# A state-space layer with a GeGLU branch on one core: last token tile projected in 384 and 128 columns, tile 0 normalised and transposed in halves, first w_gate chunk from the ScalarE queue

## Chip, cores, metric

One core of a Trainium2 chip. The metric is device time in microseconds (us) of one execution, the median of several. The profile is taken of one execution; its span runs from the first to the last instruction of the core and is about 1.8 us shorter than the device time of the same execution.

## The reference

```python
x = A_x                                   # [1, 2048, 512] bf16
xn = layernorm(x)                         # no weights, eps 1e-5
# A: diagonal complex state space, 512 states, over 2048 tokens
h_t = Lam_bar * h_{t-1} + B_bar @ xn_t ;  yA = 2 * Re(C @ h) + xn * Dskip
# B: GeGLU, hidden width 1376
yB = (gelu(xn @ w_gate) * (xn @ w_up)) @ w_down
out = x + yA + yB                         # bf16
```

## The kernel before

Tokens are handled in 4 blocks of 512 (`NB`), each of 4 tiles of 128. The kernel writes down operations with the buffers that they read and write; a list scheduler in the same file orders VectorE (DVE), ScalarE (ACT) and GpSimd (POOL) by modelled times, while TensorE (PE) and the sync queue (SP) keep the order of the program. Only the start (block 0) and the end (the last tile of block 3) matter for this change. "First projections" below means the products of block 0 with the first five chunks of 128 hidden columns of w_gate and w_up (`GU_first`). Its "second half" is the part for tiles 2 and 3. The cut below is abridged: most buffers, durations and dependencies are left out.

```python
for j in range(4):
    ld_x0(j)                                   # 128 KB each, sync queue
ld_w(WG, WGc, ins["B_w_gate"], 0)              # first chunk, 384 columns, 384 KB
ld_w(WU, WUc, ins["B_w_up"], 0)
ld_w(WG, WGc, ins["B_w_gate"], 1); ld_w(WU, WUc, ins["B_w_up"], 1)
...                                            # cut: three 1 KB parameter loads on the ScalarE queue
def LN(b, js=range(4), on_act=False, after=()):
    for j in js:
        V(bn_stats(ST[tt], X[tt]), after); V(bn_aggr(MVt[b][j], ST[tt]))
    ACT(sbq = var + eps); ACT(qb = Sqrt(sbq)); V(rq = 1 / qb)
    for j in js: V(XN[tt] = (X[tt] - mn) * rq)            # 512 columns at a time
def TR0(j, eng):                               # 4 PE transposes of tile j into one bank, one copy of 512 columns
    ...
def GU_first(fts, early, single):              # fts 0..4, early 0..2; u = 0 is w_gate, u = 1 is w_up
    for u in range(2):
        for ft in early:
            mm(ft, u, 0, 1)                    # tile 0: four matmuls of 128 columns
            if single and u == 0 and ft == 1:
                TR0(1, "A")                    # transposes of tile 1, copied by ScalarE
    for ft in early:
        for u in range(2):
            mm(ft, u, 1, 2)                    # tile 1
        evac(ft, 0)                            # Gelu on ACT, copy on ACT, product on DVE
    mm(late[0], 0, 0, 2)
    TR0(2, "V"); TR0(3, "A")
    ...                                        # cut: the other late chunks
    for ft in fts:
        for u in range(2): mm(ft, u, 2, 4)     # second half: tiles 2 and 3, 256 columns
        evac(ft, 1)
def DN(b, split=False):                        # 128 tokens x 512 columns per tile j
    ...
    for j in range(4):
        seed(j)                                # ACT puts x into the bank
        hidden(j); states(j)                   # 11 + 8 matmuls of 512 columns
        store(j)                               # DVE: bank + XD -> OUTB, then one store of 128 KB
...
nwarm = 11
PE(fwarm)                                      # nwarm matmuls of 512 columns on zeros, ahead of the first transposes
LN(0, [0], True); TR0(0, "V"); fill(4); params()     # params: one small PE transpose, then tiny operations
LN(0, [1], True, [GATE["bnag"]]); LN(0, [2, 3], True, [GATE["evT"]])
load_B(); GU_first(range(5), range(3), True)
...                                            # cut: blocks 0 to 3
GU(3, ...); DN(2); DN(3)
```

Of the kernel before, what the change touches and what calls it, by code (L numbers as in the profile page):

```python
# [61 lines left out]
class Op:  # L62
    __slots__ = ("id", "eng", "fn", "dur", "deps", "kind", "reads", "writes", "start", "finish",
                 "sem", "val", "users", "tag", "issue")

    def __init__(self, id_, eng, fn, dur, kind, reads, writes, tag):
        self.id, self.eng, self.fn, self.dur, self.kind = id_, eng, fn, float(dur), kind
        self.reads, self.writes, self.tag = reads, writes, tag
        self.deps, self.users = [], []
        self.start = self.finish = None  # L70
        self.sem = None
        self.val = None
        self.issue = DMA_ISSUE


class Sched:
# [134 lines left out]
    def _forward(self, prio):  # L211
# [13 lines left out]
        def rdy_time(op):  # L225
            return max([d.finish + LAT(d, op) for d in op.deps], default=0.0)

# [136 lines left out]
def build(nc, ins, out):  # L364
    with ExitStack() as es:
# [48 lines left out]
        XTk = [[Buf("XT%d_%d" % (b, i), "xt", 4 * b + i, 4 * b + i + 1) for i in range(4)] for b in range(NB)]  # L414
        XT0 = XTk[0]
        XTr = lambda b: XTk[b]
        WRM = A.alloc("WRM", [128], BF16)
# [52 lines left out]
        for j in range(4):  # L470
            ld_x0(j)
        ld_w(WG, WGc, ins["B_w_gate"], 0)
        ld_w(WU, WUc, ins["B_w_up"], 0)
# [43 lines left out]
        SCR = A.alloc("SCR", [1], F32)  # L517
        ACT(lambda e: e.activation(SCR.ap, HALF.ap[:, 0:1], ACTF.Sqrt), 200, [HALF, IOTJ], [SCR], "sqrt0")
        POOL(lambda e: e.memset(HR.ap, 0.0), 300, [], HRp, "hr0")
# [74 lines left out]

        def LN(b, js=range(4), on_act=False, after=()):
            j0, j1 = js[0], js[-1] + 1
            mn, sbq, qb, rq = (cols(t, b, j0, j1) for t in (MN, SBQ, QB, RQ))
            mv = Buf("MV%d_%d" % (b, j0), "sb", MVt[b][j0].lo, MVt[b][j1 - 1].hi, MV[b].ap[:, j0:j1])
            for j in js:
                tt = 4 * b + j  # L600
                V(lambda e, tt=tt: e.bn_stats(ST[tt].ap, X[tt].ap), d_dve_1x(512), [X[tt]], [ST[tt]], "bnst", after)  # L601
                GATE["bnag"] = V(lambda e, tt=tt, j=j: e.bn_aggr(MVt[b][j].ap, ST[tt].ap), D_TINY, [ST[tt]], [MVt[b][j]], "bnag")
            POOL(lambda e: e.tensor_copy(mn.ap, mv.ap[:, :, 0]), 200, [mv], [mn], "mn")
            if on_act:
                ACT(lambda e: e.activation(sbq.ap, mv.ap[:, :, 1], ACTF.Identity, bias=EPS.ap), d_act(4), [mv, EPS, SCR], [sbq], "sbq")  # L605
                ACT(lambda e: e.activation(qb.ap, sbq.ap, ACTF.Sqrt), d_act(4), [sbq], [qb], "sqrt")
            else:
                V(lambda e: e.tensor_scalar(sbq.ap, mv.ap[:, :, 1], EPS_BF16, None, ALU.add), D_TINY, [mv], [sbq], "sbq")
                POOL(lambda e: e.tensor_tensor(qb.ap, sbq.ap, HALF.ap[:, 0:j1 - j0], ALU.pow), 1100, [sbq, HALF], [qb], "pow")
            V(lambda e: e.reciprocal(rq.ap, qb.ap), 150, [qb], [rq], "rq")  # L610
            for j in js:
                tt = 4 * b + j
                xs = XN[tt % 8]
                V(lambda e, tt=tt, j=j, xs=xs: e.tensor_scalar(  # L614
                    xs.ap, X[tt].ap, mn.ap[:, j - j0:j - j0 + 1], rq.ap[:, j - j0:j - j0 + 1], ALU.subtract, ALU.mult),
                  d_dve_ts4x(512), [X[tt], mn, rq], [xs], "ln_n")

# [7 lines left out]

        def TR0(j, eng):
            if not TBANK:
                TBANK.extend([next_bank(), next_bank()])
            bank = TBANK[j % 2]
            pt = PS[bank].bitcast(BF16)  # L630

            def f(e):
                ins_ = None
                for q in range(KD):
                    ins_ = e.transpose(pt[:, 128 * q:128 * (q + 1)], XN[j].ap[:, 128 * q:128 * (q + 1)], IDN.ap)  # L635
                return ins_
            PE(f, 75.0 * KD, [XN[j], IDN], [BANK[bank]], "T0")
            dst = XNT[0].ap[:, :, 128 * j:128 * (j + 1)]
            src = pt[:, 0:512].rearrange("p (q t) -> p q t", q=KD)
            if eng == "A":  # L640
                ACT(lambda e: e.activation(dst, src, ACTF.Copy), d_act(512), [BANK[bank]], [XT0[j]], "evT")
            else:
                GATE["evT"] = V(lambda e: e.tensor_copy(dst, src), 420, [BANK[bank]], [XT0[j]], "evT")  # L643

# [67 lines left out]
        def GU_first(fts, early, single):  # L712
# [14 lines left out]

            def evac(ft, h):
                bank, c0 = banks[h][ft], 256 * h
                GATE["nh"] = kk = (GATE["nh"] + 1) % 3  # L730
                GATE["last_gelu"] = ACT(lambda e: e.activation(GG[kk].ap[:, 0:256], PS[bank][:, 0:256], ACTF.Gelu_apprx_tanh),  # L731
                                        d_act(256), [BANK[bank]], [GG[kk]], "gelu")
                ACT(lambda e: e.activation(UPB[kk].ap[:, 0:256], PS[bank][:, 256:512], ACTF.Copy),
                    d_act(256), [BANK[bank]], [UPB[kk]], "evU")
                V(lambda e: e.tensor_tensor(HTt[0][ft].ap[:, c0:c0 + 256], GG[kk].ap[:, 0:256], UPB[kk].ap[:, 0:256], ALU.mult),  # L735
                  d_dve_tt2x(256), [GG[kk], UPB[kk]], [HTt[0][ft]], "hmul")

            for u in range(2):
                for ft in early:
                    mm(ft, u, 0, 1)  # L740
                    if single and u == 0 and ft == 1:
                        TR0(1, "A")
            for ft in early:
                for u in range(2):
                    mm(ft, u, 1, 2)
                evac(ft, 0)
            late = [ft for ft in fts if ft not in early]
            mm(late[0], 0, 0, 2)
            TR0(2, "V")
            TR0(3, "A")  # L750
            for ft in late[1:]:
                mm(ft, 0, 0, 2)
# [68 lines left out]

        def DN(b, split=False):
            k2, k3 = b % 2, b % 3
            banks = [next_bank() for _ in range(4)]

            def seed(j):
                tt, bank = 4 * b + j, banks[j]
                ACT(lambda e: e.activation(PS[bank][:, :], X[tt].ap, ACTF.Copy), d_act(512), [X[tt]], [BANK[bank]], "seed")  # L828

            def mms(j, ops, last, rds):  # L830
                bank = banks[j]

                def f(e):
                    ins_ = None
                    for n, (l_, r_) in enumerate(ops):
                        ins_ = e.matmul(PS[bank][:, :], l_[:, 128 * j:128 * (j + 1)], r_, start=False,  # L836
                                        stop=last and n == len(ops) - 1, skip_group_check=True)
                    return ins_
                PE(f, d_pe([512] * len(ops)), rds + [BANK[bank]], [BANK[bank]], "DN%d" % b)

            def hidden(j):
                ops = [(HTt[k2][ft].ap[0:FROWS[ft], :], WD.ap[0:FROWS[ft], ft, :]) for ft in range(KF)]
                mms(j, ops, False, [HTt[k2][ft] for ft in range(KF)] + WDc)

            def states(j):
                ops = [(SSc[k3][s][c].ap, CT[c][s].ap) for s in range(KP) for c in range(2)]
                mms(j, ops, True, [SSs[k3][s] for s in range(KP)] + [CT[c][s] for c in range(2) for s in range(KP)])

            def store(j):
                tt, bank = 4 * b + j, banks[j]  # L850
                ko = tt % 4
                V(lambda e: e.tensor_tensor(OUTB[ko].ap, PS[bank][:, :], XD[tt].ap, ALU.add),  # L852
                  d_dve_1x(512), [BANK[bank], XD[tt]], [OUTB[ko]], "evO")
                S.dma(lambda e: e.dma_start(out[0, 128 * tt:128 * (tt + 1), :], OUTB[ko].ap),
                      128 * 1024, reads=[OUTB[ko]], is_output=True, tag="st_out")

# [5 lines left out]
            else:  # L862
                for j in range(4):
                    seed(j); hidden(j); states(j); store(j)

        nwarm = 11
        wrm4 = WRM.ap.unsqueeze(1).broadcast_to([128, 4, 128])
# [14 lines left out]

        PE(fwarm, d_pe([512] * nwarm) * 1.6, [WRM], [BANK[wb]], "warm")
        LN(0, [0], True)
        TR0(0, "V")
        fill(4)
        params()
        LN(0, [1], True, [GATE["bnag"]])
        LN(0, [2, 3], True, [GATE["evT"]])
        load_B()  # L890
# [26 lines left out]
        DN(2)  # L917
        DN(3)

# [56 lines left out]
```

## Time and profile before

| | |
|---|---|
| device time, median | 180.26 us at first (3 runs), 180.38 beside the changed kernel (6 runs) |
| span of the profiled execution | 179.05 us |
| PE busy | 173.9 us (97%) |
| first real matmul | 6.90 us |
| second half of the first projections starts | 12.48 us |
| last matmul ends | 176.03 us |

First the chain of waits of before in order of time (start, duration, engine and line, count). What is left out up to 174.35 is PE on every row, with pieces of 0.05 us of "issue" between.

```profile
12.48 4.53 PE PS L723 x40
17.00 0.05 issue
...
174.35 1.69 PE PS L836 x7
...
176.16 0.69 DVE arena L852
```

From 12.48 us to 176.04 us PE alone is the chain. So a change of the start is worth what it moves that 12.48, and a change of the end is worth what it takes off after it. The small "issue" pieces are not PE waits: before each of them one matmul record is missing, and the next start is two periods later (173.92 to 174.35 us in the last tile, where the other starts are 0.216 apart).

The timeline of PE before (start, duration, engine, line, operation, tiles, count, in brackets idle time and what ended it):

```profile
0.99 4.87 PE L873 MATMUL PS<-arena 128*128 128x512 bf16 x11 [0.99 <-DVE arena L513]
5.66 0.64 PE L635 MATMUL PS<-arena 128*128 128x128 bf16 x4
...
6.90 0.61 PE L723 MATMUL PS<-arena 128*128 128x128 bf16 x8 [0.16 <-DVE arena L610]
...
7.63 2.96 PE L723 MATMUL PS<-arena 128*128 128x128 bf16 x44
10.43 0.61 PE L635 MATMUL PS<-arena 128*128 128x128 bf16 x8
10.88 2.31 PE L723 MATMUL PS<-arena 128*128 128x256 bf16 x17
```

L873 are the warm matmuls, L635 transposes (those of tile 1, at 7.40, are left out), L723 the first projections. Merged rows hide short waits, because each matmul is drawn longer than the distance to the next one: 0.22 us at 128 columns, with starts 0.056 apart. Single matmul records of the trace show two in here: 0.12 us at 7.86 (first w_up matmul at 7.97) and 0.29 us at 12.19 (second half at 12.48). All starts of single matmuls quoted in this document are read from those records.

ScalarE before the second half, from the timeline: the Gelu table load stands in front of the Gelu pairs, and these in front of the copy of tile 3's transposes (L641), which the second half needs.

```profile
9.34 1.28 ACT L731 ACT_TABLE_LOAD   x1
...
11.70 0.63 ACT L641 ACTIVATE arena<-PS 128x512 bf16<-128x512 bf16 x1
```

The sync queue's issues, and the list of transfers (size in KB, us from issue to landing), before:

```profile
2.65 0.43 SPq L465 DMA_DIRECT2D arena<-in_B_w_gate_dram  x1
3.13 0.51 SPq L465 DMA_DIRECT2D arena<-in_B_w_up_dram  x1
```

```profile
out_dram<-arena SPq DMA_DIRECT2D x16, 128.0 KB, 1.7
arena<-in_A_x_dram SPq DMA_DIRECT2D x4, 128.0 KB, 2.2
arena<-in_B_w_gate_dram SPq DMA_DIRECT2D x1, 384.0 KB, 4.1
arena<-in_B_w_up_dram SPq DMA_DIRECT2D x1, 384.0 KB, 4.8
```

So w_gate landed at 2.65 + 4.1 = 6.75, and w_up at 3.13 + 4.8 = 7.93 us. The end of the timeline:

```profile
176.16 0.69 DVE L852 TENSOR_TENSOR arena<-PS,arena 128x512 bf16<-128x512 f32 x1 [3.41 <-PE PS L836]
176.88 0.33 SPq L854 DMA_DIRECT2D out_dram<-arena  x1
```

### The profile page before, as it was taken

The numbers are of one execution on the slowest core, as the hardware profiler recorded it, in microseconds if no ns is written. First come the engines' busy times: TensorE is split into PE (matmuls) and PEld (weight loads), VectorE is DVE, ScalarE is ACT, GpSimd is POOL, SyncE is SP. The second block draws the span as 40 slices with busy tenths as digits, with TensorE's granted clock in tenths as the row PEclk, the third lists the DMA queues.
The fourth block names the chain that finished last, engine by engine and source line by source line (L and its number), as shares of the span: only waits on it lengthen the run. The fifth ranks groups of instructions, "written<-read, shape, count | busy, mean of one in ns | idle before, by whom it ended". The sixth has DMA issues, their size and how long they took to land.

```text
span 179.0 us, 2485 instructions
## 1 busy us (share of the span) xinstructions
PE 173.9 (97%) x896; PEld 86.0 (48%) x912; DVE 156.9 (88%) x274; ACT 92.5 (52%) x178; POOL 10.1 (6%) x21
## 2 busy tenths in 40 slices
PE   7999999999999999999999999999999999999993
PEld 2687464444644444444644444444464444444441
DVE  4769997997998989988999999899999999999311
ACT  4298999976677799002667693000677700800000
POOL 3020022042000000200000000000000000000000
PEclk9999999999999999999999999999999999999999
DMA  5999918998047000002015000000001000003200
GB/s 133 291 323 171 332 38 112 160 248 262 0 88 62 0 0 0 0 29 92 0 31 102 17 4 0 29 29 29 29 4 29 0 0 0 0 0 109 71 29 29
DMA packets 26243, 12.90 MB, mean 72 GB/s; under 512 B 17560, under 2 KB 26232, under 8 KB 26232
## 3 DMA queue, kind: packets, MB, share of 16 engines
q1 hardware_dynamic: 26208, 12.75, 29.7%
q8 instruction: 7, 0.11, 0.3%
q14 instruction: 4, 0.03, 0.1%
q10 hardware_dynamic: 24, 0.00, 0.0%
HBM read 6.46 MB, written 2.10 MB: 48 GB/s over the span
## 4 chain that ended last, share of the span: by engine, by line
PE 94%; DVE 2%; ACT 1%; issue 1%; DVEq 0%
PE PS L836 36%; PE PS L798 34%; PE PS L660 15%; PE PS L772 3%; PE PS L873 3%; PE PS L723 3%; ACT L731 1%; DVE arena L601 1%; DVE arena L643 0%; DVE arena L852 0%; DVE arena L735 0%; PE PS L635 0%; DVE arena L614 0%; ACT arena L731 0%; ACT arena L605 0%
## 5 line engine op out<-in xcount | busy, mean ns | idle before, releaser
L836 PE MATMUL PS<-arena 128*128 128x512 bf16 (+1 forms) x297 | 65.8, 379 | 0.4
L798 PE MATMUL PS<-arena 128*128 128x512 bf16 x273 | 60.7, 379 | 0.4
L836 PEld LDWEIGHTS PS<-arena 128*128 128x128 bf16 (+1 forms) x304 | 29.6, 97 | 36.0
L813 ACT ACTIVATE arena<-PS 128x512 bf16<-128x512 f32 x35 | 21.0, 601 | 46.7 <-PE PS L798 33.5
L798 PEld LDWEIGHTS PS<-arena 128*128 128x128 bf16 x280 | 27.3, 98 | 32.1
L693 DVE TENSOR_TENSOR_SCAN arena<-arena 128x512 bf16<-128x512 f32 x32 | 39.0, 1253 | 0.9 <-POOL arena L541 0.9
L660 PE MATMUL PS<-arena 128*128 128x512 bf16 x126 | 28.0, 379 | 0.1
L816 ACT ACTIVATE arena<-PS 128x512 bf16<-128x512 f32 x35 | 21.0, 600 | 5.3 <-PE PS L798 5.2
L660 PEld LDWEIGHTS PS<-arena 128*128 128x128 bf16 x128 | 12.5, 98 | 14.9
L664 ACT ACTIVATE arena<-PS 128x512 bf16<-128x512 f32 x32 | 17.8, 593 | 2.6 <-PE PS L660 2.5
L852 DVE TENSOR_TENSOR arena<-PS,arena 128x512 bf16<-128x512 f32 x16 | 10.6, 680 | 9.7 <-PE PS L836 9.7
L818 DVE TENSOR_TENSOR arena<-arena 128x512 bf16<-128x512 bf16 x35 | 13.7, 415 | 2.8 <-ACT arena L816 2.6
L601 DVE BATCH_NORM_STATS2 arena<-arena 128x6 f32<-128x512 bf16 x16 | 10.3, 681 | 0.8 <-DMA arena<-in_A_x_dram 0.7
L723 PE MATMUL PS<-arena 128*128 128x256 bf16 (+1 forms) x104 | 9.6, 248 | 0.3 <-DVE arena L610 0.2
L828 ACT ACTIVATE PS<-arena 128x512 f32<-128x512 bf16 x16 | 9.4, 606 | 0.6
L680 DVE TENSOR_TENSOR arena<-arena 128x4096 bf16<-128x4096 bf16 (+1 forms) x5 | 9.3, 1856 | 0.0
L682 DVE TENSOR_TENSOR arena<-arena 128x4096 bf16<-128x4096 bf16 (+1 forms) x5 | 9.3, 1855 | 0.0
L705 DVE TENSOR_TENSOR arena<-arena 128x4096 bf16<-128x4096 bf16 x4 | 9.1, 2287 | 0.1
L706 DVE TENSOR_TENSOR arena<-arena 128x4096 bf16<-128x4096 bf16 x4 | 9.1, 2283 | 0.0
L723 PEld LDWEIGHTS PS<-arena 128*128 128x128 bf16 x104 | 8.0, 97 | 1.3 <-DVE arena L542 0.4
L614 DVE TENSOR_SCALAR arena<-arena 128x512 bf16<-128x512 bf16 x16 | 5.8, 409 | 0.4
L577 DVE SCALAR_TENSOR_TENSOR arena<-arena 128x512 bf16<-128x512 bf16 x8 | 5.5, 745 | 0.7 <-ACT arena L574 0.7
(87 smaller groups left out, 110.9 us busy)
## 6 DMA issues: line engine op xcount, KB each, us to landing
out_dram<-arena SPq DMA_DIRECT2D x16, 128.0 KB, 1.7
arena<-in_A_x_dram SPq DMA_DIRECT2D x3, 512.0 KB, 7.3
arena<-in_B_w_down_dram SPq DMA_DIRECT2D x1, 1280.0 KB, 7.0
arena<-in_A_x_dram SPq DMA_DIRECT2D x4, 128.0 KB, 2.2
arena<-in_B_w_gate_dram SPq DMA_DIRECT2D x1, 512.0 KB, 5.9
arena<-in_B_w_up_dram SPq DMA_DIRECT2D x1, 512.0 KB, 6.8
arena<-in_B_w_gate_dram SPq DMA_DIRECT2D x1, 480.0 KB, 4.4
arena<-in_B_w_up_dram SPq DMA_DIRECT2D x1, 480.0 KB, 5.1
```

Source lines behind the costliest of these rows:

```text
L601: V(lambda e, tt=tt: e.bn_stats(ST[tt].ap, X[tt].ap), d_dve_1x(512), [X[tt]], [ST[tt]], "bnst", after)
L660: ins_ = e.matmul(PS[bank][:, :], BBT[c][dk].ap[:, 128 * s:128 * (s + 1)], XNT[b].ap[:, dk, :], start=(dk == 0), stop=(dk == KD - 1))
L664: ACT(lambda e, bank=bank, k3=k3, s=s, c=c: e.activation(SSc[k3][s][c].ap, PS[bank][:, :], ACTF.Copy), d_act(512), [BANK[bank]], [SSc[k3][ ...
L693: V(lambda e, g=g, rb=rb, init=init: e.tensor_tensor_scan(g.ap, rb, g.ap, init, ALU.mult, ALU.add), d_dve_scan(512), [g, PA[RRr]] + ([CARc ...
L723: ins_ = e.matmul(PS[bank][:, q0:q0 + 128 * (j1 - j0)], W.ap[:, dk, 128 * ft:128 * (ft + 1)], XNT[0].ap[:, dk, 128 * j0:128 * j1], start=( ...
L798: ins_ = e.matmul(PS[bank][0:m, c0:c1], W.ap[:, dk, 128 * ft:128 * ft + m], XNT[b].ap[:, dk, c0:c1], start=(dk == 0), stop=(dk == KD - 1))
L813: GATE["last_gelu"] = ACT(lambda e, bg=bg, kk=kk, m=m: e.activation(GG[kk].ap[0:m, :], PS[bg][0:m, :], ACTF.Gelu_apprx_tanh), d_act(512), ...
L816: ACT(lambda e, bu=bu, kk=kk, m=m: e.activation(UPB[kk].ap[0:m, :], PS[bu][0:m, :], ACTF.Copy), d_act(512), [BANK[bu]], [UPB[kk]], "evU")
L818: V(lambda e, kk=kk, m=m, ft=ft, k2=k2: e.tensor_tensor(HTt[k2][ft].ap[0:m, :], GG[kk].ap[0:m, :], UPB[kk].ap[0:m, :], ALU.mult), d_dve_tt ...
L828: ACT(lambda e: e.activation(PS[bank][:, :], X[tt].ap, ACTF.Copy), d_act(512), [X[tt]], [BANK[bank]], "seed")
L836: ins_ = e.matmul(PS[bank][:, :], l_[:, 128 * j:128 * (j + 1)], r_, start=False, stop=last and n == len(ops) - 1, skip_group_check=True)
L852: V(lambda e: e.tensor_tensor(OUTB[ko].ap, PS[bank][:, :], XD[tt].ap, ALU.add), d_dve_1x(512), [BANK[bank], XD[tt]], [OUTB[ko]], "evO")
```

## The change

Its intent: the first real matmul sooner (w_gate from a second queue, tile 0 in halves on two engines, one warm matmul less), no ScalarE table load ahead of the copies that PE waits for, and a shorter end (the last sum and the last store cover 128 columns instead of 512).

```diff
-        ld_w(WG, WGc, ins["B_w_gate"], 0)
+        ld_w(WG, WGc, ins["B_w_gate"], 0, "scalar").nb = 900.0     # nb: not before, in the scheduler's model
         ld_w(WU, WUc, ins["B_w_up"], 0)
...
-        ACT(... ACTF.Sqrt), 200, [HALF, IOTJ], [SCR], "sqrt0")
+        ACT(... ACTF.Sqrt), 200, [HALF], [SCR], "sqrt0").nb = 1900.0
...                                   # LN(..., halves=True): variance + eps on DVE, normalised 256 columns at a time
...                                   # TR0(j, engs): two transposes and one copy of 256 columns for each engine of engs
             for u in range(2):
                 for ft in early:
                     mm(ft, u, 0, 1)
-                    if single and u == 0 and ft == 1:
+                    if single and u == 1 and ft == early[0]:
                         TR0(1, "A")
+            params()
             for ft in early:
                 for u in range(2):
                     mm(ft, u, 1, 2)
-                evac(ft, 0)
             late = [ft for ft in fts if ft not in early]
             mm(late[0], 0, 0, 2)
             TR0(2, "V")
             TR0(3, "A")
+            for ft in early:
+                evac(ft, 0, [GATE["evTA"]])    # Gelu not before the copy of tile 3
...
-                for j in range(4):
-                    seed(j); hidden(j); states(j); store(j)
+                for j in range(4):
+                    parts = ((0, D),) if tail is None or j < 3 else ((0, tail), (tail, D))
+                    for c in parts:
+                        seed(j, *c)
+                    for c in parts:
+                        hidden(j, *c); states(j, *c); store(j, *c)
-        nwarm = 11
+        nwarm = 10
...
-        LN(0, [0], True)
-        TR0(0, "V")
-        fill(4)
-        params()
-        LN(0, [1], True, [GATE["bnag"]])
-        LN(0, [2, 3], True, [GATE["evT"]])
+        LN(0, [0], True, halves=True)
+        TR0(0, "AV")
+        fill(3)
+        LN(0, [1], True, [GATE["bnag"], GATE["xn"]])
+        LN(0, [2, 3], True, [GATE["xn"]])
...
-        DN(3)
+        DN(3, tail=384)
```

More of the change, by code (lines that the diff above doesn't have):

```diff
@@ L63 @@
     __slots__ = ("id", "eng", "fn", "dur", "deps", "kind", "reads", "writes", "start", "finish",
-                 "sem", "val", "users", "tag", "issue")
+                 "sem", "val", "users", "tag", "issue", "nb")
     def __init__(self, id_, eng, fn, dur, kind, reads, writes, tag):
@@ L73, in __init__ @@
         self.issue = DMA_ISSUE
+        self.nb = 0.0
 class Sched:
@@ L225, in rdy_time @@
         def rdy_time(op):
-            return max([d.finish + LAT(d, op) for d in op.deps], default=0.0)
+            return max([d.finish + LAT(d, op) for d in op.deps] + [op.nb])
         while nleft:
@@ L415, in build @@
         XT0 = XTk[0]
+        XT0h = [Buf("XT0_0h%d" % i, "xt", 0.5 * i, 0.5 * (i + 1)) for i in range(2)]
+        XNh = [Buf("XN0h%d" % i, "sb", XN[0].lo + 512 * i, XN[0].lo + 512 * (i + 1)) for i in range(2)]
         XTr = lambda b: XTk[b]
@@ L517, in build @@
         SCR = A.alloc("SCR", [1], F32)
-        ACT(lambda e: e.activation(SCR.ap, HALF.ap[:, 0:1], ACTF.Sqrt), 200, [HALF, IOTJ], [SCR], "sqrt0")
+        ACT(lambda e: e.activation(SCR.ap, HALF.ap[:, 0:1], ACTF.Sqrt), 200, [HALF], [SCR], "sqrt0").nb = 1900.0
         POOL(lambda e: e.memset(HR.ap, 0.0), 300, [], HRp, "hr0")
@@ L593, in tables_act, with LN @@
             return ACT(lambda e: e.activation(SINT.ap, F1.ap, ACTF.Sin, scale=-SIN_SCALE), d_act(2048), [F1], [SINT], "sint", after=[t])
-        def LN(b, js=range(4), on_act=False, after=()):
+        def LN(b, js=range(4), on_act=False, after=(), halves=False):
             j0, j1 = js[0], js[-1] + 1
@@ L600, in LN @@
                 tt = 4 * b + j
-                V(lambda e, tt=tt: e.bn_stats(ST[tt].ap, X[tt].ap), d_dve_1x(512), [X[tt]], [ST[tt]], "bnst", after)
-                GATE["bnag"] = V(lambda e, tt=tt, j=j: e.bn_aggr(MVt[b][j].ap, ST[tt].ap), D_TINY, [ST[tt]], [MVt[b][j]], "bnag")
+                V(lambda e, tt=tt: e.bn_stats(ST[tt].ap, X[tt].ap), d_dve_1x(512), [X[tt]], [ST[tt]], "bnst", after[:1])
+                GATE["bnag"] = V(lambda e, tt=tt, j=j: e.bn_aggr(MVt[b][j].ap, ST[tt].ap), D_TINY, [ST[tt]], [MVt[b][j]], "bnag", after[1:])
             POOL(lambda e: e.tensor_copy(mn.ap, mv.ap[:, :, 0]), 200, [mv], [mn], "mn")
-            if on_act:
+            if halves:
+                GATE["bnag"] = V(lambda e: e.tensor_scalar(sbq.ap, mv.ap[:, :, 1], EPS_BF16, None, ALU.add), D_TINY, [mv], [sbq], "sbq")
+                ACT(lambda e: e.activation(qb.ap, sbq.ap, ACTF.Sqrt), d_act(4), [sbq, SCR], [qb], "sqrt")
+            elif on_act:
                 ACT(lambda e: e.activation(sbq.ap, mv.ap[:, :, 1], ACTF.Identity, bias=EPS.ap), d_act(4), [mv, EPS, SCR], [sbq], "sbq")
@@ L613, in LN @@
                 xs = XN[tt % 8]
-                V(lambda e, tt=tt, j=j, xs=xs: e.tensor_scalar(
-                    xs.ap, X[tt].ap, mn.ap[:, j - j0:j - j0 + 1], rq.ap[:, j - j0:j - j0 + 1], ALU.subtract, ALU.mult),
-                  d_dve_ts4x(512), [X[tt], mn, rq], [xs], "ln_n")
+                for c0, c1 in (((0, 256), (256, 512)) if halves else ((0, 512),)):
+                    w = [XNh[c0 // 256]] if halves else [xs]
+                    GATE["xn"] = V(lambda e, tt=tt, j=j, xs=xs, c0=c0, c1=c1: e.tensor_scalar(
+                        xs.ap[:, c0:c1], X[tt].ap[:, c0:c1], mn.ap[:, j - j0:j - j0 + 1], rq.ap[:, j - j0:j - j0 + 1],
+                        ALU.subtract, ALU.mult), 190 + 0.13 * (c1 - c0) if halves else d_dve_ts4x(512), [X[tt], mn, rq], w, "ln_n",
+                                   [GATE["xn"]] if c0 else ())
         def SKIP(b):
@@ L624, in build, with TR0, f @@
         TBANK = []
-        def TR0(j, eng):
+        def TR0(j, engs):
             if not TBANK:
                 TBANK.extend([next_bank(), next_bank()])
-            bank = TBANK[j % 2]
-            pt = PS[bank].bitcast(BF16)
-            def f(e):
-                ins_ = None
-                for q in range(KD):
-                    ins_ = e.transpose(pt[:, 128 * q:128 * (q + 1)], XN[j].ap[:, 128 * q:128 * (q + 1)], IDN.ap)
-                return ins_
-            PE(f, 75.0 * KD, [XN[j], IDN], [BANK[bank]], "T0")
-            dst = XNT[0].ap[:, :, 128 * j:128 * (j + 1)]
-            src = pt[:, 0:512].rearrange("p (q t) -> p q t", q=KD)
-            if eng == "A":
-                ACT(lambda e: e.activation(dst, src, ACTF.Copy), d_act(512), [BANK[bank]], [XT0[j]], "evT")
-            else:
-                GATE["evT"] = V(lambda e: e.tensor_copy(dst, src), 420, [BANK[bank]], [XT0[j]], "evT")
+            per = KD // len(engs)
+            for n, eng in enumerate(engs):
+                bank = TBANK[(j + n) % 2]
+                pt = PS[bank].bitcast(BF16)
+                def f(e, n=n, pt=pt):
+                    ins_ = None
+                    for q in range(per):
+                        k = per * n + q
+                        ins_ = e.transpose(pt[:, 128 * q:128 * (q + 1)], XN[j].ap[:, 128 * k:128 * (k + 1)], IDN.ap)
+                    return ins_
+                PE(f, 75.0 * per, [XN[j] if len(engs) == 1 else XNh[n], IDN], [BANK[bank]], "T0")
+                dst = XNT[0].ap[:, per * n:per * (n + 1), 128 * j:128 * (j + 1)]
+                src = pt[:, 0:128 * per].rearrange("p (q t) -> p q t", q=per)
+                tok = XT0[j] if len(engs) == 1 else XT0h[n]
+                if eng == "A":
+                    GATE["evTA"] = ACT(lambda e, src=src, dst=dst: e.activation(dst, src, ACTF.Copy), d_act(128 * per), [BANK[bank]], [tok], "evT")
+                else:
+                    GATE["evT"] = V(lambda e, src=src, dst=dst: e.tensor_copy(dst, src), 110 + 0.6 * 128 * per, [BANK[bank]], [tok], "evT")
         def TR(b):
@@ L726, in mm, with evac @@
                 PE(f, d_pe([128 * (j1 - j0)] * 4), [Wc[wchunk(ft)]] + XT0[j0:j1], [BANK[bank]], "GU0")
-            def evac(ft, h):
+            def evac(ft, h, after=()):
                 bank, c0 = banks[h][ft], 256 * h
@@ L731, in evac @@
                 GATE["last_gelu"] = ACT(lambda e: e.activation(GG[kk].ap[:, 0:256], PS[bank][:, 0:256], ACTF.Gelu_apprx_tanh),
-                                        d_act(256), [BANK[bank]], [GG[kk]], "gelu")
+                                        d_act(256), [BANK[bank]], [GG[kk]], "gelu", after)
                 ACT(lambda e: e.activation(UPB[kk].ap[:, 0:256], PS[bank][:, 256:512], ACTF.Copy),
@@ L820, in GU, with DN, seed, mms @@
                   d_dve_tt2x(512), [GG[kk], UPB[kk]], [HTt[k2][ft]], "hmul")
-        def DN(b, split=False):
+        def DN(b, split=False, tail=None):
             k2, k3 = b % 2, b % 3
             banks = [next_bank() for _ in range(4)]
-            def seed(j):
+            xbank = next_bank() if tail else None
+            def seed(j, c0=0, c1=D):
                 tt, bank = 4 * b + j, banks[j]
-                ACT(lambda e: e.activation(PS[bank][:, :], X[tt].ap, ACTF.Copy), d_act(512), [X[tt]], [BANK[bank]], "seed")
-            def mms(j, ops, last, rds):
-                bank = banks[j]
+                bank = banks[j] if c0 == 0 else xbank
+                ACT(lambda e: e.activation(PS[bank][:, c0:c1], X[tt].ap[:, c0:c1], ACTF.Copy), d_act(c1 - c0), [X[tt]], [BANK[bank]], "seed")
+            def mms(j, ops, last, rds, c0, c1):
+                bank = banks[j] if c0 == 0 else xbank
                 def f(e):
@@ L835, in f @@
                     for n, (l_, r_) in enumerate(ops):
-                        ins_ = e.matmul(PS[bank][:, :], l_[:, 128 * j:128 * (j + 1)], r_, start=False,
+                        ins_ = e.matmul(PS[bank][:, c0:c1], l_[:, 128 * j:128 * (j + 1)], r_[:, c0:c1], start=False,
                                         stop=last and n == len(ops) - 1, skip_group_check=True)
                     return ins_
-                PE(f, d_pe([512] * len(ops)), rds + [BANK[bank]], [BANK[bank]], "DN%d" % b)
@@ L841, in hidden, with states @@
-            def hidden(j):
+                PE(f, d_pe([c1 - c0] * len(ops)), rds + [BANK[bank]], [BANK[bank]], "DN%d" % b)
+            def hidden(j, c0=0, c1=D):
                 ops = [(HTt[k2][ft].ap[0:FROWS[ft], :], WD.ap[0:FROWS[ft], ft, :]) for ft in range(KF)]
-                mms(j, ops, False, [HTt[k2][ft] for ft in range(KF)] + WDc)
-            def states(j):
+                mms(j, ops, False, [HTt[k2][ft] for ft in range(KF)] + WDc, c0, c1)
+            def states(j, c0=0, c1=D):
@@ L846, in states, with store @@
                 ops = [(SSc[k3][s][c].ap, CT[c][s].ap) for s in range(KP) for c in range(2)]
-                mms(j, ops, True, [SSs[k3][s] for s in range(KP)] + [CT[c][s] for c in range(2) for s in range(KP)])
-            def store(j):
-                tt, bank = 4 * b + j, banks[j]
+                mms(j, ops, True, [SSs[k3][s] for s in range(KP)] + [CT[c][s] for c in range(2) for s in range(KP)], c0, c1)
+            def store(j, c0=0, c1=D):
+                tt = 4 * b + j
+                bank = banks[j] if c0 == 0 else xbank
@@ L851, in store @@
                 ko = tt % 4
-                V(lambda e: e.tensor_tensor(OUTB[ko].ap, PS[bank][:, :], XD[tt].ap, ALU.add),
-                  d_dve_1x(512), [BANK[bank], XD[tt]], [OUTB[ko]], "evO")
-                S.dma(lambda e: e.dma_start(out[0, 128 * tt:128 * (tt + 1), :], OUTB[ko].ap),
-                      128 * 1024, reads=[OUTB[ko]], is_output=True, tag="st_out")
+                ob = OUTB[ko] if c1 - c0 == D else Buf("OUTBp%d" % c0, "sb", OUTB[ko].lo + 2 * c0, OUTB[ko].lo + 2 * c1)
+                V(lambda e: e.tensor_tensor(OUTB[ko].ap[:, c0:c1], PS[bank][:, c0:c1], XD[tt].ap[:, c0:c1], ALU.add),
+                  d_dve_1x(c1 - c0), [BANK[bank], XD[tt]], [ob], "evO")
@@ L857, in DN @@
+                S.dma(lambda e: e.dma_start(out[0, 128 * tt:128 * (tt + 1), c0:c1], OUTB[ko].ap[:, c0:c1]),
+                      256 * (c1 - c0), reads=[ob], is_output=True, tag="st_out")
             if split:
```

## The prediction

> **What bounds the kernel now.** The tensor engine: the page has PE busy 173.9 of 179.0 us, and in the chain of waits PE alone makes up 12.48 to 176.04 us, with gaps of 0.05 us. The change can win only before and after that stretch.
>
> **Head, before** (timeline, PE one by one). Eleven warm matmuls of 0.427 us hold PE until 5.66, though normalised tile 0 was there at 5.19. Four transposes, spaced 107 ns (slow clock), end at 6.29; DVE copies them 6.33 to 6.75; w_gate, issued 2.65, landed 4.1 us later (6.75). The first real matmul starts at 6.90, then 56 ns per 128-column matmul. At 7.86 PE waits 0.12 us, it seems for w_up (issued 3.13, landed 4.8 us later). At 12.19 it waits 0.29 us for tiles 2 and 3, whose copies stand behind the Gelu table load (1.28 us at 9.34) and its products (11.53, and 11.70 to 12.33).
>
> **What the change does there.**
> - One warm matmul less: tile 0 transposed 0.43 us earlier; halves on two engines shorten the copies by 0.1 us. Columns ready near 6.25, not 6.75.
> - w_gate from ScalarE's queue: issued near 1.7[...]; landing estimated at 6.0 to 6.5, so the first matmul near 6.35 (-0.55). w_up is issued 0.48 us earlier: landing near 7.4.
> - The clock: the spacing goes from 107 to 56 ns at about 6.6 us. [...] So the first few matmuls run slow: +0.15 us, mostly hidden by the wait for w_up.
> - After w_up PE has about 4.5 us of fixed work: the transposes of tile 1 and of the parameters now come behind w_up (+0.33), the 0.29 us wait goes, since the copies of tiles 2 and 3 come ahead of the table load. Their normalisation hardly moves: a new wait near 10.1 of 0.1 to 0.2 us.
> - The second half of the first projections starts near 12.0 instead of 12.48: **-0.45 us**. Gelu evacuations end 0.3 us later, with 1 us of slack.
>
> **Middle.** PE 0.45 us earlier must find its inputs. I read slack of 1 us or more (last hidden products 158.5, needed 159.6; first bank of the first full Gelu free 29.0, needed 30.5). No loss.
>
> **Tail, before.** PE ends 176.04, the 512-column sum takes 0.69 us, the store is issued 176.88 and lands 1.7 us later.
> **After.** Sum of 128 columns: about 0.28 us (-0.41). The last store has a quarter of the bytes: -0.1 to -0.2. PE: 19 matmuls of 216 ns become 19 of about 163 and 19 of 56: +0.05. Net **-0.5 us**.
>
> **Sum:** 180.26 - 0.45 - 0.5 = about 179.3 us; 8 in 10: 178.8 to 179.9. Faster 0.01, within 2% 0.97, slower 0.02.
>
> **Right if** the profile shows the first projection matmul near 6.35; no PE wait above 0.1 us near 12; PE's unbroken stretch from near 12.0 to near 175.6; last sum about 0.28 us; last store landing in about 1.5 us. **Wrong in a step if** w_gate or w_up lands no earlier, last matmuls are spaced above 56 ns, or the small store lands no sooner.
>
> **Would make it wrong:** [...] DVE or ScalarE reordered so that PE waits in the middle (+0.5 us or more).

Cut at the marks: what the prediction took for granted about what decides the clock, the risk that it drew from that, and how loads from two queues share their way; no trace or run here shows these. No term of its sum is cut: 180.26 - 0.45 - 0.5 = about 179.3 us. Two estimates lost their stated reason. The +0.15, within the -0.45, is the author's estimate: it takes the 107 and 56 ns of before's trace and lets full clock come as late in the changed kernel (in before's record it came at 6.40 us). So is the 0.2 to 0.7 us that it adds to w_gate's landing: an issue near 1.7 plus the 4.1 us of before's trace gives 5.8.

## The result

| | before | changed |
|---|---|---|
| median, fast runs | 180.38 us (180.26 to 180.76, 6 runs) | 179.81 us (179.75 to 179.94, 6 runs) |
| ratio | | 0.9967, 95% interval 0.9954 to 0.998 |
| span of the profiled execution | 179.05 | 177.97 |
| first real matmul | 6.90 | 6.45 |
| first w_up matmul | 7.97 | 7.25 |
| second half of the first projections starts | 12.48 | 12.10 |
| last matmul starts / ends | 175.65 / 176.03 | 175.49 / 175.71 |

A ratio is the mean time of one kernel's fast runs over that of the other's of the same rounds, so it is not quite the ratio of the medians quoted beside it.

Something does not fit: the two traces differ by 1.08 us, the timed runs by 0.57 us. The profiled execution of before took 180.87 us, more than any of its six timed runs. One pair of traces is not enough here.

The timeline of PE in the changed kernel (L896 warm, L647 transposes, L538 parameters, L736 first projections):

```profile
0.99 4.27 PE L896 MATMUL PS<-arena 128*128 128x512 bf16 x10 [0.99 <-DVE arena L516]
5.31 0.67 PE L647 MATMUL PS<-arena 128*128 128x128 bf16 x4
...
6.45 1.19 PE L736 MATMUL PS<-arena 128*128 128x128 bf16 x16 [0.31 <-DVE arena L656]
7.48 0.39 PE L647 MATMUL PS<-arena 128*128 128x128 bf16 x4
...
8.25 0.18 PE L538 MATMUL PS<-arena 12*128 12x12 bf16 x1
8.56 1.95 PE L736 MATMUL PS<-arena 128*128 128x128 bf16 x28
10.35 0.61 PE L647 MATMUL PS<-arena 128*128 128x128 bf16 x8
```

The start is 0.45 us earlier, yet the transposes of tiles 2 and 3 begin at 10.35, against 10.43. In between, PE waits for w_up at 7.12 to 7.25, and after the parameters (8.25) about 0.2 us for ScalarE's copy of tile 1's transposes: 8.25 to 8.56 for one 12-column matmul. Only the wait at 12.2 is really gone: the copy of tile 3 now stands ahead of the table load, as the timeline of ScalarE shows.

```profile
10.99 0.60 ACT L654 ACTIVATE arena<-PS 128x512 bf16<-128x512 bf16 x1 [0.50 <-PE PS L647]
11.61 1.28 ACT L744 ACT_TABLE_LOAD   x1
12.90 0.38 ACT L744 ACTIVATE arena<-PS 128x256 bf16<-128x256 f32 x1
```

The issues, and the transfers, of the changed kernel:

```profile
1.60 0.43 ACTq L468 DMA_DIRECT2D arena<-in_B_w_gate_dram  x1
...
2.65 0.43 SPq L468 DMA_DIRECT2D arena<-in_B_w_up_dram  x1
```

```profile
arena<-in_A_x_dram SPq DMA_DIRECT2D x4, 128.0 KB, 2.9
...
arena<-in_B_w_gate_dram ACTq DMA_DIRECT2D x1, 384.0 KB, 4.2
arena<-in_B_w_up_dram SPq DMA_DIRECT2D x1, 384.0 KB, 4.6
...
out_dram<-arena SPq DMA_DIRECT2D x1, 32.0 KB, 1.4
```

The x tiles now take 2.9 us instead of 2.2, with w_gate's 384 KB issued from the second queue at 1.60 us. The end of the timeline:

```profile
174.78 0.56 DVE L871 TENSOR_TENSOR arena<-PS,arena 128x384 bf16<-128x384 f32 x1 [2.40 <-PE PS L853]
...
175.74 0.29 DVE L871 TENSOR_TENSOR arena<-PS,arena 128x128 bf16<-128x128 f32 x1 [0.41 <-PE PS L853]
```

And a line that misleads, from the chain of waits of the changed kernel. It names ScalarE (L677) as what released the projections of block 0, and so leaves PE for the whole stretch from 13.3 to 26.6:

```profile
26.17 0.46 ACT arena L677
...
26.64 6.85 PE PS L813 x31
```

But matched one by one, PE's matmuls run 0.371 us ahead of before at 16.69 and 0.372 us ahead at 163.18, with the same gaps: PE waited for nothing here. Where two releases fall together, the chain takes one of them. A shift of matched records against the other kernel shows which of them counts.

### The profile page after: what moved, and what is told of

The parts are those of the page before. It is cut to its first block, busy times and chain, and to the rows that moved or that the text cites. A ratio compares the mean times of both kernels' runs of the same rounds, so it can differ in the third digit from the quotient of the medians.

```text
span 178.0 us, 2528 instructions
## 1 busy us (share of the span) xinstructions
PE 173.3 (97%) x914; PEld 86.6 (49%) x929; DVE 157.8 (89%) x277; ACT 92.4 (52%) x179; POOL 10.2 (6%) x21
## 3 DMA queue, kind: packets, MB, share of 16 engines
q1 hardware_dynamic: 25824, 12.36, 28.4%
## 4 chain that ended last, share of the span: by engine, by line
PE 83%; ACT 5%; DVE 2%; issue 1%; ACTq 0%
PE PS L853 37%; PE PS L813 33%; PE PS L673 12%; PE PS L787 2%; ACT arena L677 2%; ACT arena L595 1%; ACT arena L596 1%; DVE arena L748 1%; DVE arena L589 1%; ACT L594 1%; DVE arena L587 0%; ACT arena L746 0%; DVE arena L871 0%; ACT arena L744 0%; ACT arena L594 0%
## 5 line engine op out<-in xcount | busy, mean ns | idle before, releaser
L853 PE MATMUL PS<-arena 128*128 128x512 bf16 (+3 forms) x317 | 65.9, 366 | 0.3
L853 PEld LDWEIGHTS PS<-arena 128*128 128x128 bf16 (+1 forms) x323 | 30.8, 98 | 35.2
L677 ACT ACTIVATE arena<-PS 128x512 bf16<-128x512 f32 x32 | 17.9, 596 | 2.2 <-PE PS L673 2.2
L871 DVE TENSOR_TENSOR arena<-PS,arena 128x512 bf16<-128x512 f32 (+2 forms) x17 | 10.9, 654 | 9.0 <-PE PS L853 8.9
L845 ACT ACTIVATE PS<-arena 128x512 f32<-128x512 bf16 (+2 forms) x17 | 9.6, 581 | 5.8 <-DVE arena L871 5.1
L736 PE MATMUL PS<-arena 128*128 128x256 bf16 (+1 forms) x104 | 9.6, 248 | 0.4 <-DVE arena L656 0.3
L736 PEld LDWEIGHTS PS<-arena 128*128 128x128 bf16 x104 | 8.1, 98 | 1.4 <-issue 0.5
L622 DVE TENSOR_SCALAR arena<-arena 128x512 bf16<-128x512 bf16 (+1 forms) x17 | 6.1, 402 | 0.4
L787 PE MATMUL PS<-arena 128*128 128x192 bf16 x64 | 5.9, 246 | 0.0
```

The lines of the kernel that those rows point to most:

```text
L677: ACT(lambda e, bank=bank, k3=k3, s=s, c=c: e.activation(SSc[k3][s][c].ap, PS[bank][:, :], ACTF.Copy), d_act(512), [BANK[bank]], [SSc[k3][ ...
L736: ins_ = e.matmul(PS[bank][:, q0:q0 + 128 * (j1 - j0)], W.ap[:, dk, 128 * ft:128 * (ft + 1)], XNT[0].ap[:, dk, 128 * j0:128 * j1], start=( ...
L845: ACT(lambda e: e.activation(PS[bank][:, c0:c1], X[tt].ap[:, c0:c1], ACTF.Copy), d_act(c1 - c0), [X[tt]], [BANK[bank]], "seed")
L853: ins_ = e.matmul(PS[bank][:, c0:c1], l_[:, 128 * j:128 * (j + 1)], r_[:, c0:c1], start=False, stop=last and n == len(ops) - 1, skip_group ...
L871: V(lambda e: e.tensor_tensor(OUTB[ko].ap[:, c0:c1], PS[bank][:, c0:c1], XD[tt].ap[:, c0:c1], ALU.add), d_dve_1x(c1 - c0), [BANK[bank], XD ...
```

## The experiments

Theory A: the profiled execution of before was a slow one. The end gives the timed gain; the start gives little in typical executions. Theory B: both traces are typical, and 0.4 us is lost outside the span. The first four runs shared 11 runs of before (180.82 us median).

### Before again

No edit.

> The kernel before, unchanged, against itself. Theory A (the profile of before fell on a slow execution: 180.87 us against a median of 180.38): this second trace has a span of 178.5 us or less, and its unbroken PE stretch (second half of the first projections) starts earlier than 12.48 us, near 12.1. Theory B (both traces are typical, and 0.4 us of the gain is lost outside the span): span 179.0 again, stretch at 12.48 again. Ratio 1.000 +- 0.001 under both.

Measured: 180.68 us, ratio 1.0002 (0.9986 to 1.0018). The span of this trace is 178.64 us, and the second half starts at 12.07. From the timeline of PE:

```profile
5.24 0.40 PE L635 MATMUL PS<-arena 128*128 128x128 bf16 x4 [0.42 <-DVE arena L614]
...
6.78 0.62 PE L723 MATMUL PS<-arena 128*128 128x128 bf16 x8 [0.81 <-DMA arena<-in_B_w_gate_dram]
```

The span expected was 178.5 or less, so that detail missed by 0.1; the stretch is where theory A put it. The same kernel, with the same instructions, has a start that differs by 0.4 us. With 11 warm matmuls tile 0 was transposed at 5.24, not 5.66, because PE's full clock came at 3.62 us in this execution (6.40 in the first) and the eleven took 3.83 us instead of 4.87; the wait of 0.29 us at 12.2 is absent.

### The last tile alone, and the start alone

```diff
 # tail alone: before.py with the changed DN, and
-        DN(3)
+        DN(3, tail=384)
 # head alone: the changed kernel with
-        DN(3, tail=384)
+        DN(3)
```

> Before with only the last token tile in 384 and 128 columns. The two traces put the tail at -0.6 us (from the first of the last tile's work on). Theory A: the tail gives all of the timed gain, -0.5 to -0.6 us, ratio 0.997. Theory B (lost outside the span, that is in the last store): -0.2 us, ratio 0.999. Trace: last sum 0.29 us, last store landing 1.4 us after issue, 19 and 19 matmuls at 162 and 56 ns.

> After without the split of the last tile. The traces put the head at -0.37 us. Theory A: against typical executions of before the head gives 0 to -0.15 us, ratio 0.999 to 1.000. Theory B: -0.37 us, ratio 0.998.

Measured: tail alone 179.84 us, ratio 0.9953 (0.9935 to 0.9971), which is -0.85 us, more than theory A's 0.5 to 0.6, which lie inside the interval. Head alone 180.66 us, ratio 1.0002 (0.9983 to 1.002): +0.03 us, with room for -0.3 to +0.4. Theory B falls, since it gave -0.2 to the tail and -0.37 to the head. The head alone's profiled execution has a row that the changed kernel's lacks:

```profile
6.37 0.83 PE L736 MATMUL PS<-arena 128*128 128x128 bf16 x12 [0.31 <-DVE arena L656]
7.93 0.40 PE L736 MATMUL PS<-arena 128*128 128x128 bf16 x4 [0.74 <-DMA arena<-in_B_w_up_dram]
```

The start is as early as ever, 6.37; then PE stands until w_up lands. Its second half starts at 12.79 us, later than in either trace of before.

With these traces the span can be taken apart. These two parts hardly change from execution to execution:

| | last tile 512 | last tile 384 + 128 |
|---|---|---|
| second half's start to the start of the last matmul | 163.17 us (4 traces) | 163.38 us (9 traces in all) |
| start of the last matmul to the end of the span | 3.40 | 2.47 to 2.49 |
| together | 166.57 | 165.86 |

So the end gains 0.71 us in every trace, and span minus 166.57 (or 165.86) tells where the second half started in the timed runs too, whose spans are listed though no trace of them is kept.

### Only w_gate on the ScalarE queue

```diff
 # before.py with
-        ld_w(WG, WGc, ins["B_w_gate"], 0)
+        ld_w(WG, WGc, ins["B_w_gate"], 0, "scalar").nb = 900.0
 # and the Sqrt no longer behind the second iota
```

> Before with only the first w_gate chunk on the ScalarE queue (and the early Sqrt no longer behind the second iota). w_gate lands near 5.8, w_up near 7.25 instead of 7.93, so the 0.12 us wait for w_up goes; but PE reaches tiles 2 and 3 as early as their normalisation allows, and the 0.29 us wait near 12.2 stays or grows. Both theories: within 0.1 us of before, ratio 0.9995 to 1.0005. If instead w_up alone set the head, -0.3 us or more.

Measured: 180.51 us, ratio 0.9997 (0.9978 to 1.0015). From the timeline of PE:

```profile
6.41 0.61 PE L724 MATMUL PS<-arena 128*128 128x128 bf16 x8 [0.28 <-DVE arena L611]
...
7.69 2.62 PE L724 MATMUL PS<-arena 128*128 128x128 bf16 x40 [0.16 <-DMA arena<-in_B_w_up_dram]
```

The first matmul starts at 6.41 although the copy of tile 0 is not in halves. w_up did not land near 7.25 as I expected, but at 7.65, and the wait for it grew from 0.12 to 0.32 us, since PE came to it sooner, at 7.37 instead of 7.86. The ratio is as expected for "w_up or the later tiles set the head", but it could not show 0.2 us.

### What sets the second half

Theory C: w_up's landing sets it, and the change made that worse, by putting the transposes of tile 1 and of the parameters behind w_up. Theory D: the normalisation of the tiles sets it, whatever w_up does. These four runs shared 11 runs of before (180.75 us median).

The changed kernel again, no edit:

> The changed kernel unchanged, as the measure for the next three. From the two traces of this head so far (changed kernel; head alone): second half of the first projections starts 4.85 us after the first w_up matmul (7.25 to 12.10; 7.93 to 12.79), whenever w_up lands. Theory C (w_up's landing sets the head, and the change put the transposes of tile 1 and of the parameters behind it): 4.85 us again, start anywhere from 12.1 to 12.8. Theory D (the normalisation of tiles 2 and 3 sets it): start 12.1 whatever w_up does. Ratio to before 0.995 to 0.997.

Measured: 179.75 us, ratio 0.997 (0.9938 to 1.0002). Its profiled execution was 181.70 us, outside of what I expected. From its timeline of PE, and its busy time by stretch (stretch and its length, PE busy and count, granted clock, DMA share, GB/s):

```profile
7.14 1.82 PE L736 MATMUL PS<-arena 128*128 128x128 bf16 x16 [0.94 <-DMA arena<-in_B_w_gate_dram]
```

```profile
6.00:7.20 1.20, 0.26 (x5) 1.00 1.02 308
7.20:8.40 1.20, 1.20 (x13) 0.52 1.07 361
8.40:10.60 2.20, 2.20 (x23) 0.50 1.09 381
10.60:12.00 1.40, 1.40 (x25) 0.98 1.42 193
```

w_gate took 5.5 us instead of 4.2, PE stood still for about 1 us, and the granted clock was half from 7.25 to 10.67 us: 3.41 us. The second half started at 13.99. The other five executions had spans of 177.9 (four) and 178.7.

Tile 1 and the parameters ahead of w_up:

```diff
             for u in range(2):
                 for ft in early:
                     mm(ft, u, 0, 1)
-                    if single and u == 1 and ft == early[0]:
-                        TR0(1, "A")
-            params()
+                if single and u == 0:
+                    params()
+                    TR0(1, "A")
```

> Changed kernel with the transposes of tile 1 and of the parameters put back ahead of the first w_up matmul. Theory C: from the first w_up matmul to the second half 4.2 to 4.5 us instead of 4.85, total 0.2 to 0.5 us under the changed kernel. Theory D: the second half starts at 12.0 to 12.1 as before, total within 0.1 us of the changed kernel.

And, with that, w_up issued before x tiles 2 and 3:

```diff
-        for j in range(4):
+        for j in range(2):
             ld_x0(j)
         ld_w(WG, WGc, ins["B_w_gate"], 0, "scalar").nb = 900.0
         ld_w(WU, WUc, ins["B_w_up"], 0)
+        for j in range(2, 4):
+            ld_x0(j)
```

> As the run before, and w_up's first chunk is issued ahead of the loads of tiles 2 and 3. w_up lands near 6.8 instead of 7.25 to 7.93, x tiles 2 and 3 near 6.0 and 6.5, still before their statistics at 7.3. Then w_up no longer gates. Theory C: second half at 12.0 in every execution, total 0.3 us under the changed kernel. Theory D: 12.0 to 12.1, equal to the changed kernel's best executions. If tiles 2 and 3 come late: 12.3 or more.

Measured: 179.84 us, ratio 0.9952 (0.9939 to 0.9964), and 179.76 us, ratio 0.9946 (0.9935 to 0.9958). In these traces w_up landed at 2.65 + 4.4 = 7.05 and 1.65 + 5.0 = 6.65, before PE asked for it (7.69 and 7.63, right behind the transposes of tile 1). Even so the second half started at 12.14 and 12.04 (4.45 and 4.41 us after the first w_up matmul), no earlier than the changed kernel's 12.10. In the second of the two runs x tiles 2 and 3 landed only at 7.04 and 7.34, without harm: their statistics began at 7.33, against 7.31 in the changed kernel. From its chain of waits (L738 projections, L540 parameters, L649 transposes):

```profile
6.53 0.83 PE PS L738 x12
7.36 0.11 PE PS L540
7.47 0.33 PE PS L649 x4
7.80 0.67 PE PS L738 x12
...
8.49 1.95 PE PS L738 x28
```

From the first real matmul on, PE alone is the chain. So there is a floor, an earliest start that w_up does not set, at about 12.0 to 12.1, as theory D had it. Its reason is not theory D's: no transpose waits more than 0.05 us for the normalisation of tiles 2 and 3. What is left is the order of PE's work behind the first real matmul (6.58 and 6.53), with about 0.2 us for the parameters and, by the single records, a wait of 0.18 us for the copy of tile 1's transposes (before 8.54 and 8.49). The gain against the changed kernel that theory C promised came only from its late executions: all ten spans of these two kernels are 177.9 to 178.2.

The last tile in 256 and 256 columns:

```diff
-        DN(3, tail=384)
+        DN(3, tail=256)
```

> Changed kernel with the last tile cut 256 and 256. If the tail's gain is the size of the last sum and of the last store: last sum 0.42 us instead of 0.29, last store landing 1.55 us after issue instead of 1.4, PE the same (38 matmuls at 109 ns = 4.1 us), so 0.2 us over the changed kernel. If any split gives it: equal.

Measured: 180.15 us, ratio 0.9974 (0.996 to 0.9989), 0.4 us over the changed kernel's median of the same rounds; of that the end explains 0.23, and the rest is the spread of the start. Its last sum took 0.42 us, its last store landed 1.5 us after issue; from the start of the second half to the start of the last matmul it takes 163.33 us, and 2.76 us from there to the end, together 166.09 against 165.86. So the size of the last part is what counts, as expected.

### Forcing w_up late

```diff
-        ld_w(WU, WUc, ins["B_w_up"], 0)
         ld_w(WG, WGc, ins["B_w_gate"], 1)
+        ld_w(WU, WUc, ins["B_w_up"], 0)
```

> Changed kernel with w_up's first chunk issued behind w_gate's second one (512 KB). Theory C: w_up lands 1.3 to 1.8 us later (8.6 to 9.0), PE waits for it from 7.1, and the second half starts 4.85 us later again, near 13.6: 1.3 to 1.8 us over the changed kernel, and more if the tensor clock falls back in that pause, as in the one slow execution of the changed kernel (pause of 1.1 us, then 107 ns spacing for 3.4 us). Theory D: below 0.5 us.

Measured (11 runs of before in the same rounds, 180.86 us median): 181.59 us in the median of three fast runs, ratio 1.0034 (1.0011 to 1.0057), one more execution at 184.19 with a mean clock of 0.981. That is 1.56 us over the changed kernel's median of the same rounds (180.03, below), inside theory C's 1.3 to 1.8. w_up landed 6.0 us after its issue. From the timeline of PE:

```profile
6.69 0.85 PE L736 MATMUL PS<-arena 128*128 128x128 bf16 x12 [0.28 <-DMA arena<-in_B_w_gate_dram]
9.20 0.40 PE L736 MATMUL PS<-arena 128*128 128x128 bf16 x4 [1.66 <-DMA arena<-in_B_w_up_dram]
```

Full clock was kept through this pause (granted 1.00 in every stretch from 7.2 to 14 us). The second half started at 14.05: 1.95 us later than in the first trace of the changed kernel for a first w_up matmul 1.95 us later. Theory C holds above the floor, one for one. Side by side, read from the single matmul records:

| order of PE | trace | first w_up matmul | second half | between |
|---|---|---|---|---|
| changed | changed kernel | 7.25 | 12.10 | 4.86 |
| changed | head alone | 7.93 | 12.79 | 4.85 |
| changed | last tile 256 + 256 | 7.18 | 12.06 | 4.88 |
| changed | changed kernel, third time | 7.72 | 12.58 | 4.86 |
| changed | w_up late | 9.20 | 14.05 | 4.85 |
| changed | changed kernel, second time (half clock) | 8.32 | 13.99 | 5.67 |
| before | before | 7.97 | 12.48 | 4.51 |
| before | before again | 7.86 | 12.07 | 4.21 |
| before | tail alone | 7.67 | 12.28 | 4.62 |
| before | w_gate alone | 7.69 | 11.99 | 4.30 |

Behind w_up the old order needs 4.21 us when nothing else waits, and the new order 4.85 whenever the clock is full.

The changed kernel a third time, and the two reorderings a second time:

> The changed kernel a third time. If w_up's landing spreads it: most executions at 177.9 to 178.1 us, one or two at 178.5 or more; ratio 0.995 to 0.998.

> The run with tile 1, the parameters and w_up's first chunk ahead, a second time. If its evenness is real (five executions between 177.9 and 178.0 us), again all within 0.2 us; ratio to before 0.9945 to 0.9955.

Measured: 180.03 us, ratio 0.9949 (0.993 to 0.9968), spans 178.4, 178.5, 178.4, 178.0, 177.9, 178.1; and 179.85 us, ratio 0.9944 (0.9926 to 0.9962), spans 177.9 to 178.1 with one of 178.6. The evenness that I took from the first five executions did not hold fully, and three of the changed kernel's six were at 178.4 or 178.5, where I had expected most at 177.9 to 178.1. The profiled one of the reordered kernel has the second half at 12.22, with its first real matmul at 6.59, so the floor itself is 12.0 to 12.2. The late executions of the changed kernel have a row like this in the timeline of PE (third time):

```profile
6.58 0.83 PE L736 MATMUL PS<-arena 128*128 128x128 bf16 x12 [0.31 <-DVE arena L656]
7.72 0.40 PE L736 MATMUL PS<-arena 128*128 128x128 bf16 x4 [0.32 <-DMA arena<-in_B_w_up_dram]
```

A last try to lower the floor: w_up's first chunk ahead of x tiles 2 and 3, tile 1's transposes ahead of w_up with the parameters left behind it, and one group between the transposes of tiles 2 and 3:

```diff
             TR0(2, "V")
+            mm(late[0], 1, 0, 2)
             TR0(3, "A")
```

> Changed kernel with w_up's first chunk issued ahead of the loads of tiles 2 and 3, the transposes of tile 1 ahead of the first w_up matmul (the parameters' stay behind it), and one group of w_up matmuls between the transposes of tiles 2 and 3. In the run with the first two of these the floor of the head was the normalisation: transposes of tile 1 at 7.40 behind the parameters', of tile 3 at 10.50. Here tile 1 at 7.29, tile 3 no longer waited for: second half at 11.9 instead of 12.04 to 12.10; span 177.8; 0.5 us under the changed kernel's mean where that one has late executions, 0.1 us under its best.

Measured: 179.93 us, ratio 0.9951 (0.9928 to 0.9974), spans 177.8, 179.1, 178.3, 177.8, 178.3, 177.9. The profiled execution has the second half at 11.99, not 11.9, and still the earliest of the kernels with the changed order or a variant of it; the mean is not better. All three reorderings beat before clearly. That any of them beats the changed kernel is not shown: in the same rounds 0.9946 stands against 0.997, and 0.9944 and 0.9951 against 0.9949, with intervals that overlap.

## Why the prediction was right or wrong

The total was right: 179.3 us predicted with 178.8 to 179.9, 179.81 measured. Its two halves were not: the end was under-sized and the start over-sized. That the total held is in part luck: the predicted gain was 0.95 us and the rounds of the result gave 0.57, 0.09 us inside the range; two errors of opposite sign partly cancelled. The gain also depends on the rounds, since before's start varies: between medians of the same rounds it was 1.00 and 0.83 us when the changed kernel ran again.

- **What bounds the kernel, and "no loss" in the middle: right.** In all traces with the same last tile the time from the second half to the last matmul agrees within 0.01 us, wherever the second half starts. Moving PE 0.4 us either way meets no new wait.
- **The end, predicted -0.5: right in mechanism, under-sized.** Measured -0.71 in every trace, and -0.85 timed (interval -0.5 to -1.2). The terms: the last sum 0.69 to 0.29 us (-0.40, predicted -0.41); the store's landing after the sum's end 1.72 to 1.46 us (-0.26, predicted -0.1 to -0.2); PE's matmuls 162.5 and 56 ns apart (+0.05 at the last end, predicted +0.05); and the sum starts 0.04 us after the last matmul's modelled end instead of 0.14 (-0.1, not predicted). The store and that gap are the mis-sized terms.
- **The start, predicted -0.45: this is the step that failed.** The prediction let w_up land near 7.4, with about 4.5 us of fixed work behind it and a wait of 0.1 to 0.2. The runs show w_up at 7.1 to 8.1 and 4.85 us from its first matmul to the second half. The pair of traces shows -0.37 and seems to confirm it. Timed, head alone gives +0.03 (from -0.3 to +0.4). From the spans, worked out as above: before's second half starts at 12.43 in the median and 12.36 in the mean of 33 executions (spans listed beside the later runs); the changed kernel's at 12.14 and 12.33 of 18. A typical execution gains about 0.3 us and late ones give it back.
  - *First matmul near 6.35:* 6.37 to 6.69 in nine traces with the new head or a variant of it, 7.14 in one where w_gate came late. Right as a place, but PE's later work hung on w_up wherever that came late; only with w_up early does it hang on this matmul. The slow first matmuls (+0.15) were absent in the changed kernel's first trace, where full clock came at 4.94.
  - *One warm matmul less makes tile 0's transposes 0.43 us earlier:* only where the clock comes up late. It came up between 3.62 and 6.75 us in the traces that record it; in before again 11 warm matmuls were over in time and the transposes stood at 5.24.
  - *w_up issued 0.48 us earlier lands near 7.4:* from issue to landing it took 4.5 to 5.4 us (mean 4.95) in the five traces with the changed head, against 4.5 to 4.8 (mean 4.67) in the three with the old loads. So it landed at 7.59 instead of 7.79 in the mean: less than half of the earlier issue arrived. What took the rest is not shown, since the ranges overlap and the traces are few. The x tiles too took longer with w_gate's load on a second queue: 2.8 to 3.2 us from issue to landing, against 2.1 to 2.3 with one queue (medians of the four tiles, in eight and three traces).
  - *Work behind w_up grows by 0.33 and the wait of 0.29 goes:* the work grew by 0.64 (4.85 against 4.21). The transposes of tile 1 (0.22) and of the parameters (0.20, read where nothing waits behind them) are about 0.43 of it. The rest, about 0.2, is a wait for ScalarE's copy of tile 1's transposes, which used to pass under the w_up matmuls. I had expected a wait of 0.1 to 0.2 us, but at 10.1, for tile 3. And the 0.29 us that go were a property of one execution: over the 4.21 us without a wait the four traces with the old order show 0.29, 0, 0.40 and 0.09. In the two with 0.29 and 0.40 full clock came late, at 6.40 and 5.75 us, and the chain of waits leads from the warm matmuls over tile 0's transposes and the table load to the second half. In the other two full clock came at 3.62 and 4.39, and the chain starts with the issues and the transfer of w_gate or w_up. So in these four traces the wait that the change takes away is large only where full clock came late.
- **The clock: it cost time once, in another place.** One execution of the changed kernel lost full clock again after two pauses of PE and took 181.70 us. That the pauses are the cause is not shown: with w_up late PE paused 1.66 us (7.54 to 9.20), after full clock had come at 6.75, and kept it. Whether the change makes this more frequent is open: it was 1 of 18 executions.

What stays open: why the landing spreads between executions of the same kernel, by 0.9 us for w_up and 1.5 for w_gate in the three traces of the changed kernel, and why the clock fell in one trace and stayed full in another with a longer pause. No run here takes the transfers themselves apart.

## What to carry to other kernels

An operand's wait at the start is worth moving only if it is the last of them: find the one that the engine waits for last (here w_up, and w_gate's first matmul only once w_up comes early), and do not put work behind it that could have filled the wait. A profile is one execution; where the start hangs on transfers, take the same kernel two or three times and compare fixed intervals between records, which agree to 0.01 us, before believing a difference of 0.4 us in spans. At the end of this kernel the size of the last piece counted (its sum took 0.69, 0.42 and 0.29 us at 512, 256 and 128 columns, its store landed in 1.70, 1.52 and 1.44), so make the piece that follows the last matmul small.

## Other figures of these traces

- Full clock came 2.6 to 5.8 us after the first matmul at 0.99 us (at 3.62 in before again, at 6.75 with w_up late).
- Ahead of the last matmul the clock fell to half in one trace, the changed kernel's second, from 7.25 to 10.67 us. PE had paused twice before that, 0.65 us before the transposes and 0.94 us before the first real matmul. But with w_up late the clock stayed full through a pause of 1.66 us (7.54 to 9.20), so the length of a pause alone does not decide here.
- Starts of matmuls at full clock, each with its own weight load, are 56 ns apart at 128 columns, 109 at 256, 162.5 at 384, and 216 at 512.
- In the changed kernel's first trace the Gelu table load took 1.28 us, began 0.02 us after the copy before it and was followed 0.01 us later by the first Gelu.
- The stores at the end landed in 1.70, 1.62, 1.52 and 1.44 us for 128, 96, 64 and 32 KB, with rows of 1024, 768, 512 and 256 B, about 0.09 us less for each 32 KB.
- From issue to landing, the same load spread between executions: w_gate 3.9 to 5.5 us and w_up 4.4 to 5.4 us, in six traces with the same loads issued at the same times (1.6 and 2.65 us).
